# A gate on one queue: later loads issued once the first column's moments are computed

## The chip, the cores and the metric

The kernel runs on one core of a Trainium2 chip. The metric is the time of one execution on the device in microseconds, as the median of several executions. The profile is of one execution; its times are microseconds from the first instruction of the program.

## What is computed

The input x has 2048 rows of 512 bfloat16 values. Each row is normalised (mean and variance over its 512 values), and the result feeds two branches whose outputs are added to x:

```python
x = A_x
xn = _layernorm(x, axis=-1)
return x + _A_ref(xn, A_w_r, A_w_i) + _B_ref(xn, B_w_gate, B_w_up, B_w_down)
```

Branch A is a spectral filter: a real two-dimensional Fourier transform of xn, a product with the complex weights w_r + i w_i, and the inverse transform. Branch B is a gated feed-forward layer: g = xn w_gate and u = xn w_up (512 to 1792), h = gelu(g) * u, and h w_down (1792 to 512).

## The kernel before

The 2048 rows are held as 16 columns of 128 rows, one row of a column in each partition; row 16 p + c lies in partition p of column c. `x_t` holds the columns as loaded, `xn` the normalised ones, and `xnT` their transposes, which the matrix products read. `Wg_sb` and `Wu_sb` hold the gate and up weights as four blocks of 128 inputs by 1792 outputs.

For a column, DVE computes the moments (`f_stats`, L339, then `f_mean`, L342, into `mv`). The reciprocal root of the variance is made on ACT and DVE for columns 0 and 1, and on POOL for the others. DVE or ACT then writes `xn` (L345, L452). Columns 0 to 3 are transposed on TensorE (`f_T`, L351, into `tp`) and copied to `xnT` by DVE or ACT (L354); the other columns are transposed by DMA (L455).

The matrix products of branch B come in units (function `unit`): a unit covers some columns and some blocks of 128 outputs. It makes `g_ps` and `u_ps` on TensorE (L490; L498 for the gate half of the first unit), the gelu on ACT (L503) and the product on DVE (L508). The first two units take columns 0 and 1 one at a time with output blocks 0 to 3, which need the outputs 0 to 512 of both weight matrices; the third and fourth take columns 0 and 1 together with blocks 4 to 7, which need the outputs 512 to 1024. The products of branch A (`bp`, `dp`, `ep`, `gp`, `yp`) are spread between later units, and the products with `Wd_sb` (`y_ps`, L817) close the program. Before the first transposes TensorE runs 37 matmuls on a zero tile (L320), and six more (L324) before the first unit; their results are not used.

The order on each engine is fixed before the program runs. Most work is registered with `plan.add`, with an engine, an estimated duration, dependencies and a key; a small simulation (`Plan.order`) picks the next operation by earliest start and key, and the operations are then issued in that order. The loads at the top are not in the plan: they are issued directly, in the order of the text, on the queue of SP, and stand ahead of everything that the plan puts on SP. `load_x(c0, n)` (L273) loads n columns of x, `load_w(T, a, b)` (L277) loads outputs a to b of one weight matrix. At most eight DMAs on this queue have a semaphore of their own: a ninth waits for the landing of the first, and so on.

`first_two` registers the work on columns 0 and 1. Its helper `v` adds a DVE operation that follows the one added before it. Its first operations are:

```python
stats(0)
mean(0)
stats(1)

recip(0)
xn_(0, 0)
```

Of the kernel before, what the change touches and what calls it, by code (L numbers as in the profile page):

```python
# [19 lines left out]
NC = 16  # L20
NG = 8
NE = 4
DF = 1792
# [111 lines left out]
class Plan:  # L135
# [6 lines left out]
    def add(self, eng, occ, fn, deps=(), key=0.0, lat=None, slack=0.0, t_min=0.0, acq=(), rel=(), after=None):  # L142
        lat = occ + 0.25 if lat is None else lat
        op = Op(len(self.ops), eng, occ, lat, fn, [d for d in deps if d is not None], key, slack, t_min, acq, rel,
                after)
        self.ops.append(op)
        return op
# [54 lines left out]
def kernel(  # L202
# [11 lines left out]
    nc = tc.nc  # L214
    const_np, ccols, rf_np, ri_np, idx_np = _tables()
    cap = nc.inline_tensor(const_np, name="spec_consts").ap()
    rf_d = nc.inline_tensor(rf_np, name="spec_rf").ap()
# [12 lines left out]
    x_t = pc.tile([P, NC, D], BF16, name="x_t", tag="x_t")  # L230
    CT = pc.tile([P, const_np.shape[1]], BF16, name="CT")
    Wg_sb = pc.tile([P, NE, DF], BF16, name="Wg_sb")
    Wu_sb = pc.tile([P, NE, DF], BF16, name="Wu_sb")
# [4 lines left out]
    RF_t = pc.tile([P, NC, P], BF16, name="RF_t", tag="RF")  # L238
    late = {}
    W = 257  # L240
    TW = pc.tile([P, 2, 17, W], BF16, name="TW", tag="TW")
    TR, TI = TW[:, 0], TW[:, 1]
# [5 lines left out]
    def load_consts(first, last):  # L248
        a, b = ccols[first][0], sum(ccols[last])
        nc.sync.dma_start(out=CT[:, a:b], in_=cap[:, a:b])  # L250


    def load_x(c0, n, eng=nc.sync):
        eng.dma_start(out=x_t[:, c0:c0 + n, :], in_=x_v[:, c0:c0 + n, :])

    def load_w(a, b, eng=nc.sync):
        nc.sync.dma_start(out=Wg_sb[:, :, a:b], in_=wg_v[:, :, a:b])
        eng.dma_start(out=Wu_sb[:, :, a:b], in_=wu_v[:, :, a:b])
# [25 lines left out]
    nc.sync.dma_start(out=idx_t[:], in_=nc.inline_tensor(idx_np, name="spec_rows").ap())  # L284
    load_w(Wg_sb, 0, 512)
    load_w(Wu_sb, 0, 512)
    load_x(2, 2)
    load_w(Wg_sb, 512, 1024)
    load_w(Wu_sb, 512, 1024)
    load_x(4, 2)  # L290
    load_x(6, 2)
    load_w(Wg_sb, 1024, DF)
    load_w(Wu_sb, 1024, DF)
    load_x(8, 2)
    load_x(10, 2)
    for c in range(0, NC, 8):
        nc.sync.dma_start(out=RF_t[:, c:c + 8], in_=rf_d.rearrange("p (c k) -> p c k", c=NC)[:, c:c + 8])
    load_x(12, 2)
    load_x(14, 2)
    load_consts("F0", "L0")  # L300
    load_consts("I0", "M0")
    for T, w_in in ((TR, A_w_r), (TI, A_w_i)):
        rows = w_in.rearrange("(kb a h g) k -> h kb a (g k)", kb=NC, h=2, a=8)
        Tf = T.rearrange("p j k -> p (j k)")
        for h in range(2):
            nc.sync.dma_start(out=Tf[64 * h:64 * h + 64, W:8 * W], in_=rows[h, :, 0:4, W:8 * W])

    LAND = {0: 2.9, 1: 3.6, 2: 8.4, 3: 8.4}
    LAND.update({c: 11.5 if c < 8 else 17.5 if c < 12 else 20.5 for c in range(4, NC)})
# [18 lines left out]
    add = plan.add  # L328
    V, A, T_ = nc.vector, nc.scalar, nc.tensor
# [7 lines left out]
    def f_stats(c):  # L337
        tiles["st", c] = st = pw.tile([P, V.BN_STATS_DIM], F32, name="stats", bufs=4)
        V.bn_stats(out=st[:], in_=x_t[:, c, :])  # L339

    def f_mean(c):
        V.bn_aggr(out=mv[:, c, :], in_=tiles["st", c][:])  # L342

    def f_norm_v(c, o, w):
        V.tensor_scalar(out=xn[:, c, o:o + w], in0=x_t[:, c, o:o + w], scalar1=mv[:, c, 0:1],  # L345
                        scalar2=rstd[:, c:c + 1], op0=ALU.subtract, op1=ALU.mult)

    def f_T(c, e0, n):
        tiles["T", c, e0] = tp = ps.tile([P, n, P], BF16, name="tp", tag="S", bufs=4)
        for e in range(n):  # L350
            T_.transpose(tp[:, e], xn[:, c, (e0 + e) * P:(e0 + e + 1) * P], ident)  # L351

    def f_Tc(c, e0, n, copy=V.tensor_copy):
        copy(out=xnT[0][:, e0:e0 + n, c, :], in_=tiles["T", c, e0][:])  # L354
# [19 lines left out]
    def first_two():  # L374
        o = {}

        def v(k, fn, occ, deps=(), lat=None, t_min=0.0):
            o[k] = add("DVE", occ, fn, [o[d] for d in deps], key=-2000 + len(o), lat=lat, t_min=t_min,
                       after=o.get("last"))
            o["last"] = o[k]  # L380

        def T(c, h):
            o["T", c, h] = add("PE", 0.12, lambda: f_T(c, 2 * h, 2), [o["xn", c, h]], key=-2000 + 2 * c + h,
                               lat=0.36, acq=("S",))

        def xn_(c, h):
            v(("xn", c, h), lambda: f_norm_v(c, 256 * h, 256), 0.27, [("recip", c)], lat=0.4)

        def stats(c):
            v(("stats", c), lambda: f_stats(c), 0.6, t_min=LAND[c], lat=0.7)  # L390

        def mean(c):
            v(("mean", c), lambda: f_mean(c), 0.17, [("stats", c)])
            o["root", c] = add("ACT", 0.31, lambda: A.activation(
                out=rstd[:, c:c + 1], in_=mv[:, c, 1:2], func=AF.Sqrt, bias=eps_t[:], scale=1.0),
                [o["mean", c]], key=-2000 + c)

        def recip(c):
            v(("recip", c), lambda: V.reciprocal(out=rstd[:, c:c + 1], in_=rstd[:, c:c + 1]), 0.15, [("root", c)])

        stats(0)
        mean(0)
        stats(1)

        recip(0)
        xn_(0, 0)
        mean(1)
        xn_(0, 1)
        T(0, 0)
        T(0, 1)  # L410
        add("PE", 0.33, spin_on, [o["T", 0, 1]], key=-1500, lat=0.33, after=o["T", 0, 1])
        table = add("ACT", 1.3, lambda: None, [o["root", 1]], key=-1500, lat=1.3)
        v("copy0", lambda: f_Tc(0, 0, 2), 0.25, [("T", 0, 0)], lat=0.4)
        o["copy0"].rel = ("S",)
        xT_op[0, 0] = o["copy0"]
        recip(1)
        v("copy1", lambda: f_Tc(0, 2, 2), 0.25, [("T", 0, 1)], lat=0.4)
        o["copy1"].rel = ("S",)
        xT_op[0] = o["copy1"]
        xn_op[0] = o["xn", 0, 1]  # L420
        v("xn1", lambda: f_norm_v(1, 0, D), 0.33, [("recip", 1)], lat=0.45)
        t = add("PE", 0.23, lambda: f_T(1, 0, NE), [o["xn1"]], key=-1998, lat=0.45, acq=("S",))
        o["t"] = t
        v("copyt", lambda: f_Tc(1, 0, NE), 0.5, ["t"])
        o["copyt"].rel = ("S",)
        xT_op[1] = o["copyt"]
        xn_op[1] = o["xn1"]

    ROOT = 1.1
    first_two()  # L430

    def moments(c, key):
# [448 lines left out]
```

## Time and profile before

| | |
|---|---|
| median of six runs | 178.75 us (178.48 to 179.11) |
| the profiled execution, its own time | 178.66 us |
| its span, first to last instruction | 177.0 us |
| TensorE busy | 173.0 us |
| DVE busy | 116.2 us |
| ACT busy | 96.0 us |
| POOL busy | 17.2 us |
| bytes moved by DMA | 19.35 MB |

In the profile PE is TensorE's matmuls and PEld its weight loads, which overlap them. SPq is the instruction stream of SP, which issues the loads. A group line gives the program's line, the engine, the operation and its tiles. In a timeline the first two numbers are start and length of a row, and the bracket says how long the engine stood idle before it and what ended that. The profiled execution's own time is 1.66 us longer than its span; that part lies outside the instructions.

The first loads were issued by SP at 0.80 (columns 0 and 1 of x), 1.71 (a table of row numbers), 2.18 (gate weights 0 to 512) and 2.65 (up weights 0 to 512). Columns 2 and 3 followed at 3.20, the second gate quarter (512 to 1024) at 3.75 and the second up quarter at 4.23.

### The profile page before, as it was taken

How to read it: one execution, taken by the hardware profiler on the slowest of the kernel's cores; microseconds unless marked ns; L12 is line 12 of the kernel's file. 1: busy time of each engine (PE TensorE's matmuls, PEld its weight loads, DVE VectorE, ACT ScalarE, POOL GpSimd, SP SyncE). 2: the span in 40 equal slices, each digit the busy share in tenths (PEclk: the TensorE clock that was granted, in tenths of full speed). 3: DMA queues.
4: the chain of work that ended last, by engine and by line, in shares of the span. 5: the costliest groups of instructions: out<-in, count | busy, mean ns of one | idle time of the engine just before them, and what ended most of it. 6: DMA issues, size and time to landing. Idle time of an engine off the chain costs nothing.

```text
span 177.0 us, 3132 instructions
## 1 busy us (share of the span) xinstructions
PE 173.0 (98%) x1145; PEld 97.1 (55%) x1145; DVE 116.2 (66%) x255; ACT 96.0 (54%) x170; POOL 17.2 (10%) x38
## 2 busy tenths in 40 slices
PE   7999999999999999999999999999999999999993
PEld 7898845455545554555455455454445445444463
DVE  3678999987434599979899999643516325345333
ACT  4442489799736988898899964362112111211200
POOL 1020340505760000000000000000000000000000
PEclk9999999999999999999999999999999999999999
DMA  3999999335716802211201520200132221221212
GB/s 82 357 374 378 376 188 143 67 63 70 254 35 228 309 0 59 59 30 35 59 19 43 147 51 15 59 0 4 59 90 89 77 75 61 89 88 60 78 45 59
DMA packets 21871, 19.35 MB, mean 109 GB/s; under 512 B 8480, under 2 KB 20000, under 8 KB 21856
## 3 DMA queue, kind: packets, MB, share of 16 engines
q1 hardware_dynamic: 21440, 17.84, 36.5%
q0 software_dynamic: 416, 1.32, 2.6%
q8 instruction: 9, 0.15, 0.4%
q14 instruction: 6, 0.05, 0.1%
HBM read 13.38 MB, written 2.10 MB: 87 GB/s over the span
## 4 chain that ended last, share of the span: by engine, by line
PE 94%; DMA 3%; SPq 1%; issue 0%; DVE 0%
PE u_ps L490 27%; PE y_ps L817 27%; PE g_ps L490 27%; DMA Wu_sb<-in_B_w_up_dram 3%; PE bp L577 2%; PE yp L768 2%; PE gp L738 2%; PE dp L635 2%; PE y_ps L821 2%; PE ep L644 2%; SPq L273 0%; PE tp L351 0%; SPq L277 0%; SPq L284 0%; DVE y_sb L824 0%
## 5 line engine op out<-in xcount | busy, mean ns | idle before, releaser
L490 PE MATMUL u_ps<-xnT,Wu_sb 128*128 128x512 bf16 (+2 forms) x272 | 57.3, 341 | 0.1
L490 PE MATMUL g_ps<-xnT,Wg_sb 128*128 128x512 bf16 (+2 forms) x256 | 56.2, 349 | 0.0
L817 PE MATMUL y_ps<-Wd_sb,hT 128*128 128x512 bf16 (+2 forms) x252 | 51.1, 355 | 0.0
L508 DVE TENSOR_TENSOR hT<-u_ps,ge 128x512 bf16<-128x512 f32 x56 | 38.5, 689 | 18.2 <-PE u_ps L490 14.5
L503 ACT ACTIVATE ge<-g_ps 128x512 bf16<-128x512 f32 x56 | 33.7, 602 | 24.0 <-PE g_ps L490 21.3
L490 PEld LDWEIGHTS <-Wu_sb 128*128 128x128 bf16 x272 | 24.9, 98 | 20.9 <-DMA Wu_sb<-in_B_w_up_dram 0.2
L817 PEld LDWEIGHTS <-hT 128*128 128x128 bf16 x252 | 23.2, 98 | 22.4
L490 PEld LDWEIGHTS <-Wg_sb 128*128 128x128 bf16 x256 | 24.0, 98 | 20.6
L774 ACT CAST yf<-yp 128x512 bf16<-128x512 f32 x16 | 9.3, 587 | 40.5 <-PE yp L768 40.5
L824 DVE TENSOR_TENSOR y_sb<-y_ps,y_sb 128x512 bf16<-128x512 f32 (+2 forms) x18 | 11.1, 631 | 30.0 <-PE y_ps L821 30.0
L649 ACT CAST E<-ep 64x512 bf16<-64x512 f32 x32 | 18.6, 580 | 1.4 <-PE ep L644 1.0
L339 DVE BATCH_NORM_STATS2 stats<-x_t 128x6 f32<-128x512 bf16 x16 | 10.4, 677 | 2.5 <-DMA x_t<-in_A_x_dram 2.4
L452 ACT ACTIVATE xn<-x_t,nb,rstd 128x512 bf16<-128x512 bf16 x12 | 9.5, 815 | 1.0 <-POOL nb L370 1.0
L547 ACT CAST ds<-dp 128x512 bf16<-128x512 f32 x16 | 9.2, 598 | 0.8 <-PE dp L635 0.8
L547 ACT CAST Gs<-gp 128x512 bf16<-128x512 f32 x16 | 8.7, 592 | 0.6 <-PE gp L738 0.5
L547 ACT CAST Bs<-bp 128x512 bf16<-128x512 f32 x16 | 8.3, 609 | 0.5 <-PE bp L577 0.5
L780 DVE TENSOR_TENSOR lv<-yf 128x512 bf16<-128x512 bf16 x16 | 6.1, 422 | 1.5 <-ACT yf L774 0.6
L768 PEld LDWEIGHTS <-Gs 128*128 128x128 bf16 x64 | 4.8, 98 | 3.5
L787 DVE TENSOR_TENSOR yt<-lv 128x512 bf16<-128x512 bf16 x16 | 6.1, 421 | 0.3
L821 PE MATMUL y_ps<-yt,RI_t 128*128 128x512 bf16 (+2 forms) x18 | 6.1, 355 | 0.0
L768 PE MATMUL yp<-CT,Gs 128*128 128x128 bf16 x64 | 6.0, 219 | 0.0
L559 DVE TENSOR_TENSOR A<-xn 128x1024 bf16<-128x1024 bf16 x8 | 5.2, 677 | 1.0 <-ACT xn L452 1.0
(65 smaller groups left out, 120.3 us busy)
## 6 DMA issues: line engine op xcount, KB each, us to landing
F<-F SPq DMA_DIRECT2D x32, 64.0 KB, 2.0
y_sb<-in_A_x_dram SPq DMA_DIRECT2D x16, 128.0 KB, 2.1
out_dram<-y_sb SPq DMA_DIRECT2D x15, 128.0 KB, 1.7
x_t<-in_A_x_dram SPq DMA_DIRECT2D x7, 256.0 KB, 8.8
Wd_sb<-in_B_w_down_dram SPq DMA_DIRECT2D x1, 1792.0 KB, 7.6
Wg_sb<-in_B_w_gate_dram SPq DMA_DIRECT2D x2, 512.0 KB, 5.4
Wu_sb<-in_B_w_up_dram SPq DMA_DIRECT2D x2, 512.0 KB, 6.4
Wg_sb<-in_B_w_gate_dram SPq DMA_DIRECT2D x1, 768.0 KB, 10.1
```

The source lines that it names most:

```text
L339: V.bn_stats(out=st[:], in_=x_t[:, c, :])
L452: xn_op[c] = add("ACT", 0.72, lambda c=c: A.activation(out=xn[:, c, :], in_=x_t[:, c, :], func=AF.Identity, bias=nb[:, c:c + 1], scale=rst ...
L490: T_.matmul(b[name][:, f], lhsT=W_[:, e, (f0 + f) * P:(f0 + f + 1) * P], rhs=rhs[:, e, :], start=(e == 0), stop=(e == NE - 1))
L503: A.activation(out=b["ge"][:], in_=b["g_ps"][:], func=AF.Gelu_apprx_tanh)
L508: V.tensor_tensor(out=hT_of(sb, f0, m, o, w), in0=b["u_ps"][:], in1=b["ge"][:], op=ALU.mult)
L547: A.copy(out=o, in_=i)
L649: A.copy(out=b["E"][64 * h:64 * h + 64, r], in_=b["ep", h][64 * r:64 * r + 64])
L768: T_.matmul(t[:, q], lhsT=late["G"][:, q, c0 + j], rhs=IQ[q], start=(q == 0), stop=(q == 3), skip_group_check=True)
L774: A.copy(out=b["yf"][:, j], in_=b[j][:])
L817: T_.matmul(b[o][:], lhsT=hT_of(sb, f, 1, cl * P, P)[:, 0], rhs=Wd_sb[:, f, o:o + w], start=(f == 0), stop=False)
L821: T_.matmul(b[o][:], lhsT=late["RI"][:, c, :], rhs=late["yt"][:, c, o:o + w], start=False, stop=True)
L824: V.tensor_tensor(out=b["y"][:, o:o + w], in0=b[o][:], in1=b["y"][:, o:o + w], op=ALU.add)
```

## The change

All loads behind the first quarter of the up weights are moved into a function, unchanged and in the same order. That function is registered in the plan as one SP operation, which depends on a new DVE operation: a memset of one element of `x_t`, in column 2, placed between the mean of column 0 and the statistics of column 1. Column 2 is the first thing that the moved loads write, so the first of them waits for the memset. In the instruction streams DVE has one instruction more, the load of columns 2 and 3 has one wait more, and all else stands in the order of before.

```diff
     load_w(Wg_sb, 0, 512)
     load_w(Wu_sb, 0, 512)
-    load_x(2, 2)
-    load_w(Wg_sb, 512, 1024)
-    load_w(Wu_sb, 512, 1024)
-    load_x(4, 2)
-    load_x(6, 2)
-    load_w(Wg_sb, 1024, DF)
-    load_w(Wu_sb, 1024, DF)
...
+
+    def later_loads():
+        load_x(2, 2)
+        load_w(Wg_sb, 512, 1024)
+        load_w(Wu_sb, 512, 1024)
+        load_x(4, 2)
+        load_x(6, 2)
+        load_w(Wg_sb, 1024, DF)
+        load_w(Wu_sb, 1024, DF)
+        load_x(8, 2)
+        load_x(10, 2)
+        for c in range(0, NC, 8):
+            nc.sync.dma_start(out=RF_t[:, c:c + 8], in_=rf_d.rearrange("p (c k) -> p c k", c=NC)[:, c:c + 8])
+        load_x(12, 2)
+        load_x(14, 2)
+        load_consts("F0", "L0")
+        load_consts("I0", "M0")
+        for T, w_in in ((TR, A_w_r), (TI, A_w_i)):
...
         stats(0)
         mean(0)
+        v("gate", lambda: V.memset(x_t[0:1, 2, 0:1], 0.0), 0.06, lat=0.1)
+        add("SP", 9.0, later_loads, [o["gate"]], key=-1000)
         stats(1)
```

More of the change, by code (lines that the diff above doesn't have):

```diff
@@ L286 @@
     load_w(Wu_sb, 0, 512)
-    load_x(2, 2)
-    load_w(Wg_sb, 512, 1024)
-    load_w(Wu_sb, 512, 1024)
-    load_x(4, 2)
-    load_x(6, 2)
-    load_w(Wg_sb, 1024, DF)
-    load_w(Wu_sb, 1024, DF)
[L294 to L306, printed above, removed]
+    def later_loads():
[15 more added lines that the diff above has]
+        for T, w_in in ((TR, A_w_r), (TI, A_w_i)):
+            rows = w_in.rearrange("(kb a h g) k -> h kb a (g k)", kb=NC, h=2, a=8)
+            Tf = T.rearrange("p j k -> p (j k)")
+            for h in range(2):
+                nc.sync.dma_start(out=Tf[64 * h:64 * h + 64, W:8 * W], in_=rows[h, :, 0:4, W:8 * W])
     LAND = {0: 2.9, 1: 3.6, 2: 8.4, 3: 8.4}
```

## The prediction

> **What bounds the kernel now.** I read the page first, for which engine carries the span and what the chain that ended last consists of.
>
> ```profile
> span 177.0 us, 3132 instructions
> PE 173.0 (98%) x1145; PEld 97.1 (55%) x1145; DVE 116.2 (66%) x255; ACT 96.0 (54%) x170; POOL 17.2 (10%) x38
> ...
> PE 94%; DMA 3%; SPq 1%; issue 0%; DVE 0%
> ```
>
> TensorE is the bound. Ahead of its work in the chain stands one DMA piece, 3% of the span. The chain in order of time, cut to 0 to 14 us, shows where that lies:
>
> ```profile
> 2.18 0.43 SPq L277
> 2.61 0.04 issue
> 2.65 5.20 DMA Wu_sb<-in_B_w_up_dram
> 7.85 0.05 issue
> 7.89 1.07 PE u_ps L490 x16
> ```
>
> So the first quarter of the up weights (issued at 2.65, landed at 7.85) lets TensorE go at 7.89, and from there the chain holds almost only TensorE work. A microsecond won or lost there moves the end one for one; what lands later without stopping TensorE costs nothing. The timeline says how much TensorE really lost there, and what is next to stop it:
>
> ```profile
> 7.86 0.42 DVE L354 COPY xnT<-tp 128x512 bf16<-128x512 bf16 x1 [1.21 <-PE tp L351]
> 7.89 0.90 PEld L490 LDWEIGHTS <-Wu_sb 128*128 128x128 bf16 x16 [0.24 <-DMA Wu_sb<-in_B_w_up_dram]
> ...
> 8.61 0.69 DVE L339 BATCH_NORM_STATS2 stats<-x_t 128x6 f32<-128x512 bf16 x1 [0.32 <-DMA x_t<-in_A_x_dram]
> ...
> 10.53 1.68 PEld L490 LDWEIGHTS <-Wg_sb 128*128 128x128 bf16 x16
> ```
>
> The weight loader idled 0.24 us before the first up matmul: that is all an earlier landing can give back. The next two loads on the path are the ones that the change puts behind its gate: x columns 2 and 3 (DVE starts on them at 8.61) and the second quarter of the gate weights (first used at 10.53). Then the DMA issues, each taken alone, with microseconds from issue to landing; x_t was issued at 3.20 and Wg_sb at 3.75:
>
> ```profile
> x_t<-in_A_x_dram SPq DMA_DIRECT2D x1, 256.0 KB, 5.4
> Wg_sb<-in_B_w_gate_dram SPq DMA_DIRECT2D x1, 512.0 KB, 6.6
> ```
>
> They land at 8.60 and 10.35: DVE takes the x columns at once, and the gate weights have 10.53 - 10.35 = 0.18 us to spare. Last the windows, to see whether issue or bandwidth sets those landings (last two columns: busy share of the DMA engines, and GB/s):
>
> ```profile
> 4.00:5.00 1.00, 1.00 (x12) 0.91 (x9) 0.88 (x3) 0.30 (x1) 0.00 (x0) 1.00 0.79 248
> 5.00:6.00 1.00, 0.90 (x8) 0.53 (x7) 0.83 (x5) 0.63 (x2) 0.00 (x0) 1.00 1.08 377
> 6.00:7.00 1.00, 1.00 (x15) 0.96 (x14) 0.65 (x4) 0.95 (x1) 0.00 (x0) 1.00 1.07 380
> 7.00:8.00 1.00, 0.93 (x17) 0.76 (x15) 0.14 (x1) 0.36 (x1) 0.00 (x0) 1.00 1.06 340
> ```
>
> From about 4.5 us the DMA engines are full. The windows from 1 to 7 us move 20 + 233 + 50 + 248 + 377 + 380 = 1308 kB. The x columns 0 and 1 and the first gate and up quarters are 2 x 128 + 2 x 512 KB = 1311 kB. So those bytes, and hardly any of a load behind them, had moved by 7.0: the loads go through in the order of their issue. What stands behind the gate is not touched by the engines before about 7.0, and Wg_sb's second quarter not before 7.0 + 262 kB / 377 GB/s = 7.7.
>
> **The change part by part.**
>
> The gate: one DVE memset of one element. The 128x1 memsets (L264, L266) take 0.06 us, the 128x64 one 0.11. It stands between the first column's mean (3.80 + 0.18 = 3.98) and the second column's statistics, which start at 4.09 because their column lands only at 1.25 + 2.8 = 4.05. The 0.11 us hole covers it: 0 on DVE. Without that cover it would push the DVE chain of columns 0 and 1 by 0.06 to 0.11 us; that chain feeds transposes and matmuls that are done 0.24 us before the up weights come, so still 0 at the end.
>
> The wait: SP finishes the up issue at 2.65 + 0.51 = 3.16 and now waits for the memset's end, about 4.04 to 4.09. The trace has one such release, a 1x1 memset on POOL that ends at 53.01 with the DMA behind it issued at 53.05, so 0.04 us more: x columns 2 and 3 go out at about 4.10 instead of 3.20, 0.9 us later. Queued behind on SP, in unchanged order, are the second quarters of Wg and Wu, the other x loads, the weight thirds, RF_t, CT, TW, and then the transposes (from 22.28) and everything later. At the spacing of before, Wg_sb's second quarter goes out at 3.75 + 0.9 = 4.65 and Wu_sb's at 5.13. The issues are back in step by 10: at 6.67 and 8.04 SP sat 1.33 and up to 1.83 us on single issues where earlier ones took 0.43 to 0.68, held by a full queue, and the RF_t issue at 10.39 waits for a landing anyway. No other engine issues a load in this stretch, and all other instructions keep their order.
>
> What the 0.9 us costs: the delayed loads must reach the engines before these run dry at 7.0. For the time from issue to first bytes the nearest row is Wd_sb, issued into an idle queue at 53.05: the window 53.50:54.00 shows 0 GB/s and 54.00:54.50 shows 68, so between 0.95 and 1.45 us; 285 GB/s is reached in 55.00:55.50, within 2.45 us. x columns 2 and 3, out at 4.10, have bytes ready by 5.55 and need them at 7.0: 1.4 us to spare. Wg_sb's second quarter has them by 6.1 and needs them at 7.7: 1.6 us to spare. By this, 0 us lost. The other end is the whole 0.9 us sliding through to the landings, priced below. I take 0, since the engines keep a backlog of 1311 - 325 (moved by 4.1) = about 990 kB, 2.6 us at 377 GB/s, against 0.9 of delay.
>
> What it gains: between 0 and 0.24 us. Less traffic behind the up weights could let them land earlier, but the sum above shows hardly any of that traffic moving before 7.0, and it will be queued again by 5.55. I take 0.
>
> The Trainium skill, "DMA: Bandwidth & Descriptors", section "Rules for kernel authors", speaks against the change: issue a DMA early and wait for it late, so that its fixed cost overlaps. By that rule alone holding the issue back costs up to the 0.9; this trace covers it with a backlog. The same page, section "Specifications", gives about 0.6 us to first byte for DMAs of this path; by it the sum is 0 as well, with more to spare; the 0.95 to 1.45 us here are longer, and they are what counts. Its section "Queues, rings and completion order" says that each DMA engine consumes descriptors in ring order, which is what the 1308 of 1311 kB show here; by it the gain is 0.
>
> Sum: 178.66 us (the profiled execution, span 177.0 and 1.66 around it) + 0 + 0 - 0 = 178.66. The median of the six runs is 0.09 higher; I forecast 178.7.
>
> **The rivals.**
>
> The delay slides through (slower). If bytes come more than 3.05 us after issue (7.7 - 4.65), or the queue doesn't catch up, the second gate quarter lands up to 0.9 later, 11.25, and the weight loader, which wants it at 10.53, waits 0.72. The x columns land at 9.50, their normalised columns move from 12.19 (11.46 + 0.73) to up to 13.09, and the transposes, which TensorE would by then start at 12.22 + 0.72 = 12.94, wait another 0.15. Price 0.72 to 0.87, say 0.8: 179.5. It decides once the second gate quarter is over 0.18 us late. For it: DVE and TensorE take both loads almost as they land. Against it: the backlog.
>
> The up weights land earlier (faster). For it: some DMA engines run ahead, and the bytes from 6.5 to 7.5 belong partly to x columns 2 and 3 while the last up rows land at 7.85. Gain at most the 0.24 us gap, then the copy at 7.86 to 8.28, the x columns and the gate weights (0.18 to spare) come next: 178.42, or 178.5 against the median. That is 0.13%, less than can be told.
>
> The change doesn't do what it says: it holds back issues, and the transfers behind them were waiting for the engines anyway. That is my forecast.
>
> **How the numbers follow.** A measurement of this kernel can tell about 0.2% (0.36 us): the six runs lie from 178.48 to 179.11, 0.15% under to 0.20% over their median. Hidden, 178.7: 0.72. Earlier landing, 178.5: 0.13. Slide through, 179.5: 0.12. Something else, either way: 0.03. By cases: hidden gives 0.64 same and 0.04 on each side by scatter; earlier landing 0.05 faster, 0.08 same; slide 0.11 slower, 0.01 same; the rest 0.01 each. Faster 0.10, same 0.74, slower 0.16. The range runs from the earlier landing less 0.2 us of scatter, 178.3, to the slide's 179.5.
>
> **What the next profile would show.** Right: the L273 issue of columns 2 and 3 near 4.1; the up weights landing at 7.8 to 7.9 with a PEld gap of about 0.24; x columns landing near 8.6; the second gate quarter by 10.5; the windows 5 to 10 still at 340 to 380 GB/s; RF_t issued near 10.4. Wrong: a window between 6 and 9 under 300 GB/s, a PEld gap on Wg_sb before 10.6 or on xn near 12.2 (slide), or an up landing before 7.7 with the gap gone (gain).

## The result, and the profile after

The changed kernel is slower: 179.7 us in the median of 28 runs, against 179.02 us of the kernel before on the same chips; ratio 1.0049, 95% interval 1.0035 to 1.0062. Executions at a lower granted clock are left out of the ratio, as one of the changed kernel at 0.991. The ratio is worth 0.9 us. The median lies outside the range of 178.3 to 179.5; carried over to the 178.75 us that the forecast started from, the ratio gives 179.6, just outside as well. The profiled execution took 179.51 us, of which 177.8 are the span.

The page first, as before:

```profile
span 177.8 us, 3133 instructions
PE 173.3 (97%) x1145; PEld 97.1 (55%) x1145; DVE 116.0 (65%) x256; ACT 96.0 (54%) x170; POOL 17.6 (10%) x38
...
PE 88%; DMA 5%; DVE 2%; ACT 2%; issue 1%; SPq 0%
```

TensorE works as long as before (173.3 against 173.0 us), in a span 0.8 us longer. The chain now holds more DMA, and DVE and ACT pieces that it did not have. Its first part, in order of time:

```profile
0.80 2.13 DMA x_t<-in_A_x_dram
2.93 0.02 issue
2.95 0.71 DVE stats L341
3.66 0.02 issue
3.68 0.18 DVE mv L344
3.86 0.03 DVE stats L341
3.90 0.02 issue
3.92 0.34 SPq L273
4.26 0.04 issue
4.30 6.75 DMA Wg_sb<-in_B_w_gate_dram
11.04 0.05 issue
11.09 1.92 PE g_ps L494 x16
```

The gate stands in the chain: first column, statistics, mean, memset (the piece at 3.86 carries the line of the statistics that overlap it), the released issue at 3.92, the second gate quarter, landed at 11.04 instead of 10.34. The weight loader's list of waits says what that costs, and shows a second loss in another place:

```profile
PEld L494 <- DMA Wg_sb<-in_B_w_gate_dram: 0.5, 1, 0.5
PEld L494 <- DMA Wu_sb<-in_B_w_up_dram: 0.4, 1, 0.4
...
PEld L581 <- issue: 0.2, 1, 0.2
```

The first is the loader's wait ahead of the third unit, which TensorE starts at 11.09 instead of 10.59: **0.50 us**. The second is not a loss: the up weights land at 7.85 as before, and the loader is ready 0.2 us sooner. The third lies at 41.2 us, in branch A. The 33rd to 48th `bp` matmuls, in the timelines of TensorE of the kernel before (first line) and after:

```profile
39.70 1.06 PE L577 MATMUL bp<-RF_t,xf 128*128 128x128 bf16 x16
```

```profile
40.22 1.39 PE L581 MATMUL bp<-RF_t,xf 128*128 128x128 bf16 x16
```

They begin 0.52 us later, which is the first loss, and last **0.33 us** longer. 0.50 + 0.33 = 0.83 of the 0.85 us between the spans (177.80 and 176.95 unrounded); what follows is late by the same amount to the end.

**The first loss** is in the transfers. Windows (busy share of the DMA engines, GB/s):

```profile
6.00:7.00 1.00, 1.00 (x16) 0.74 (x14) 0.35 (x2) 0.65 (x1) 0.00 (x0) 1.00 1.21 357
7.00:8.00 1.00, 0.73 (x14) 0.56 (x12) 0.34 (x1) 0.56 (x1) 0.00 (x0) 1.00 0.79 235
8.00:9.00 1.00, 1.00 (x20) 1.00 (x20) 0.09 (x1) 0.04 (x1) 0.00 (x0) 1.00 0.93 284
9.00:10.00 1.00, 1.00 (x22) 1.00 (x20) 0.67 (x2) 0.11 (x1) 0.00 (x0) 1.00 1.06 353
```

Against 340 GB/s before, 7 to 8 us moves 235. The next window moves 284; before it was:

```profile
8.00:9.00 1.00, 1.00 (x20) 1.00 (x20) 0.68 (x2) 0.24 (x1) 0.00 (x0) 1.00 1.03 347
```

Taken together the engines had not run dry: the 2 KB packets of x columns 2 and 3 begin at 6.70 us in both traces. But the busy share falls with the rate (0.79 and 0.93 against 1.06 and 1.03). Added up from the start and length of each packet in the trace, about 17 packets are in flight at any time from 5.5 to 6.5 us in both kernels. From 6.75 to 8.75 us, in steps of 0.25, it is 13.4 to 15.7 after and 15.7 to 17.3 before. With fewer than 16 in flight, some of the 16 engines have nothing to move; that begins where the first loads come to their end. And single packets are slow: ten of the 2 KB packets take over 200 ns, the longest 1045 ns (median 84 ns); before, three do, the longest 324 ns.

A load has landed when the last of the 16 steps that its semaphore makes has come. For the second gate quarter the ninth step comes at 10.14 us (9.81 before) and the last at 11.04 (10.34): the load is not only later, its parts lie further apart. So the columns land at 9.31 instead of 8.59 (DVE's wait for them is now 1.25 us, 0.32 before), and the gate quarter behind them 0.7 us late.

**The second loss** starts on DVE at 25 us. Timeline of DVE, kernel before and after:

```profile
24.33 0.66 DVE L559 TENSOR_TENSOR A<-xn 128x1024 bf16<-128x1024 bf16 x1
25.23 0.69 DVE L508 TENSOR_TENSOR hT<-u_ps,ge 128x512 bf16<-128x512 f32 x1 [0.24 <-PE u_ps L490]
```

```profile
24.85 0.66 DVE L563 TENSOR_TENSOR A<-xn 128x1024 bf16<-128x1024 bf16 x1
26.17 0.69 DVE L512 TENSOR_TENSOR hT<-u_ps,ge 128x512 bf16<-128x512 f32 x1 [0.66 <-ACT xn L456]
```

The sum of xn's halves begins 0.52 us late, the product that writes `hT` 0.94. Its `u_ps` was done at 25.64 and its gelu at 25.42, so by its waits it could start near 25.74, 0.1 us after `u_ps` as before; it starts 0.43 us after that. The releaser named, ACT's `xn`, is only what happened to end last: the programs wait for the same counts in both kernels, apart from DVE's own count, one higher (for this product ACT's 17th step, which came with the gelu at 25.43; `xn` is the 18th). Nor is it the POOL instruction of 1.04 us that runs meanwhile: it begins at 25.17 before and at 25.68 after, and before, the product started beside it without a delay. From this product the delay goes to the statistics behind it, to POOL's `nb`, to ACT's `xn` (groups: 1.0 us idle before, 1.8 after, all on `nb`), and to ACT's copies of `bp` out of PSUM, 0.94 us late. A `bp` matmul then waits for a buffer.

### The profile page after: what moved, and what is told of

Same layout as the page of the kernel before. It is cut to its first block, busy times and chain, and to the rows that moved or that the text cites. A ratio compares the mean times of both kernels' runs of the same rounds, so it can differ in the third digit from the quotient of the medians.

```text
span 177.8 us, 3133 instructions
## 1 busy us (share of the span) xinstructions
PE 173.3 (97%) x1145; PEld 97.1 (55%) x1145; DVE 116.0 (65%) x256; ACT 96.0 (54%) x170; POOL 17.6 (10%) x38
## 4 chain that ended last, share of the span: by engine, by line
PE 88%; DMA 5%; DVE 2%; ACT 2%; issue 1%; SPq 0%
PE y_ps L821 27%; PE g_ps L494 25%; PE u_ps L494 25%; DMA Wg_sb<-in_B_w_gate_dram 4%; PE yp L772 2%; PE gp L742 2%; PE dp L639 2%; PE y_ps L825 2%; PE ep L648 2%; PE bp L581 1%; DMA x_t<-in_A_x_dram 1%; ACT Bs L551 1%; DVE hT L512 1%; DVE A L563 1%; ACT ge L507 1%
```

## The experiments

"Landing distance" below is the time from the landing of the first up quarter to that of the second gate quarter, from each profile: 2.49 us before, 3.19 us after. The bp stretch is the start of the 33rd to that of the 48th bp matmul: 0.84 us before, 1.17 us after.

**First set: the wait, its place, and the loads behind it.**

e1, gate opened at the start:

```diff
+        v("gate", lambda: V.memset(x_t[0:1, 2, 0:1], 0.0), 0.06, lat=0.1)
+        add("SP", 9.0, later_loads, [o["gate"]], key=-1000)
         stats(0)
         mean(0)
-        v("gate", ...)
-        add("SP", 9.0, later_loads, [o["gate"]], key=-1000)
```

> The same memset and the same wait, but the memset stands ahead of the first statistics, where DVE has nothing to do, so the gate is open at about 1.1 us and no load is held back. Theory S (a load's bytes follow its issue by a fixed few us, so the held-back issue slides through to the landing): issue of x columns 2 and 3 at 3.20, landing at 8.6, second gate quarter landing at 10.3 to 10.4, time as before within 0.2%. Rival W (the memset or the wait itself costs, whenever it opens): landings of 9.3 and 11.0 as in the changed kernel, time 0.4 to 0.5% over before.

Measured: 1.0016 (1.0002 to 1.0029). The x columns go out at 3.20, landing distance 2.49: nothing left of the first loss. The bp stretch is 1.16 us: the second loss stays. So the first loss comes from when the loads go out, and the second comes with gate, wait or memset.

e2, gate behind `xn_(0, 1)`:

```diff
         mean(1)
         xn_(0, 1)
+        v("gate", lambda: V.memset(x_t[0:1, 2, 0:1], 0.0), 0.06, lat=0.1)
+        add("SP", 9.0, later_loads, [o["gate"]], key=-1000)
```

> The gate moves from behind the first column's mean to behind the second half of its normalisation, so the held-back loads go out at about 5.4 instead of 3.9. Theory S (slide, one for one): x columns 2 and 3 land about 1.5 later than in the changed kernel, near 10.8, the second gate quarter near 12.5, TensorE stands 1.8 to 2.1 us before it, time about 1.5 us over the changed kernel, 181.2. Rival R (the DMA engines run empty once after the up weights and pay one restart of fixed length, whatever the delay): landing of the second gate quarter under 11.5, time within 0.4 us of the changed kernel.

Measured: 1.0036 (1.0021 to 1.0051). The x columns go out at 5.80, 1.9 us later than in the changed kernel, and land at 9.10, sooner than there, although the up quarter itself landed late, at 8.20; landing distance 3.05. A delay of 2.6 us costs no more than one of 0.7: the delay does not slide through. Windows of e2:

```profile
7.00:8.00 1.00, 1.00 (x20) 0.99 (x18) 0.00 (x0) 0.17 (x2) 0.00 (x0) 1.00 1.05 236
8.00:9.00 1.00, 0.92 (x17) 0.76 (x15) 0.42 (x1) 0.58 (x1) 0.00 (x0) 1.00 0.87 216
```

The same dip, from 7 to 8 us at a busy share of 1.05, as high as in the kernel before: here the slow packets count for more. Eighteen of the 2 KB packets take over 200 ns, the longest 975.

e3, the three next loads ahead of the gate, gate (on x column 4) behind `copy1`:

```diff
+    load_x(2, 2)
+    load_w(Wg_sb, 512, 1024)
+    load_w(Wu_sb, 512, 1024)
     def later_loads():
-        load_x(2, 2)
-        load_w(Wg_sb, 512, 1024)
-        load_w(Wu_sb, 512, 1024)
```

> x columns 2 and 3 and the second quarters of both weights go out ahead of the gate; the gate holds the loads of x columns 4 on and opens behind the second transpose copy, near 6.4, so x columns 4 and 5 go out about 1.4 later than the 4.96 of before, with over 1.5 MB queued ahead of them. Theory S with a fixed latency of 3 to 3.7 us from issue to first bytes: bytes at about 10, when the queue gets there, so no dry window: x columns 4 and 5 land at 12.4 to 12.8, windows 9 to 13 stay over 340 GB/s, time as before within 0.2%. Rival D (every delay of an issue slides through, however much is queued): landing near 13.9, a window between 9 and 12 under 300 GB/s; the time may still be that of before, since these columns are first used at 15.4.

Measured: 1.0029 (1.0001 to 1.0058). x column 4 goes out 1 us later than before (5.97) and lands at 12.53, before 12.48; landing distance 2.21. By the landings, a held load further back costs nothing. The bp stretch is 1.16, so the second loss is there.

e7, x columns 2 and 3 free, the rest held until `xn_(0, 1)`:

```diff
+    load_x(2, 2)
     def later_loads():
-        load_x(2, 2)
...
+        v("gate", lambda: V.memset(Wg_sb[0:1, 0, 512:513], 0.0), 0.06, lat=0.1)
```

> x columns 2 and 3 are issued ahead of the gate (3.20 as before); the gate opens behind the second half of the first normalisation, so the second gate quarter goes out near 5.8 instead of 3.75, 2 us late. Theory R: the restart moves from x columns 2 and 3 to the second gate quarter, which has 0.18 us to spare; x columns land at 8.6, the gate quarter at 10.6 to 11.2, time 0.1 to 0.5% over before. Theory S (slide): gate quarter at 12.4, time 1.1% over before. If a backlog of the x columns alone covers 2 us, landing 10.4 and time as before.

Measured: 1.0013 (1.0000 to 1.0025). The second gate quarter goes out at 5.49 instead of 3.75, about 2 us ahead of its first packets, and lands at 10.30 (before 10.34); landing distance 2.20, no 2 KB packet over 109 ns, and windows without a dip:

```profile
7.00:8.00 1.00, 0.94 (x17) 0.77 (x14) 0.02 (x1) 0.24 (x1) 0.00 (x0) 1.00 1.05 364
8.00:9.00 1.00, 0.86 (x16) 0.86 (x17) 0.59 (x2) 0.36 (x1) 0.00 (x0) 1.00 1.09 351
```

So, of the loads held in these runs, only the one directly behind the up quarter must not be late. It isn't the number of bytes still queued: 805 kB were when e7's quarter went out, and 1017 kB when the x columns of the changed kernel did.

e5, the changed kernel again. 

> The changed kernel itself, on one chip with the three variants beside it, for a size to compare them with: 0.35 to 0.6% over before. Theory R (restart: what costs is that the DMA engines come to the end of the up weights with nothing fetched behind them, a cost of some 0.7 us that hardly grows with the delay) and theory S (slide) both expect that.

Measured: 1.0062 (1.0031 to 1.0093), landing distance 3.17, bp stretch 1.15: both losses repeat.

e6, no gate, no memset; two small loads hold SP instead:

```diff
     load_w(Wu_sb, 0, 512)
+    for k in range(2):
+        tiny = pc.tile([1, 3], I32, name=f"tiny{k}")
+        nc.sync.dma_start(out=tiny[:], in_=...)
     load_x(2, 2)
```

> The kernel before with no gate, no memset and no wait, but two loads of 12 bytes each issued between the up quarter and x columns 2 and 3, so that SP issues these at about 4.0 to 4.1, as late as in the changed kernel. Theories R and S: the delay alone is enough, slow windows at 7 to 9 us (under 300 GB/s), second gate quarter landing near 11, time 0.3 to 0.6% over before. Rival W (the memset or the wait costs): time within 0.2% of before.

Measured: 1.0057 (1.0036 to 1.0077), landing distance 3.85, more than the gate's. The bp stretch is 0.84: without the memset there is no second loss.

e8, the loads as before, and only a memset into a scratch tile where the gate memset stands. 

> The kernel before with the one-element memset in the same place, into a tile that nothing reads; loads issued directly as before. Theories R and S: time within 0.15% of before. Rival W, memset half: over 0.2% slower.

Measured: 1.0017 (1.0004 to 1.0030), bp stretch 1.15. One memset of one element costs 0.3 us, and not where it stands. The loads go out as before, and yet this profile has a landing distance of 2.83 us and windows of 312 and 289 GB/s from 7 to 9 us: a part of the dip is scatter from one execution to the next. DVE at 25 us in e8, with nothing else changed:

```profile
24.43 0.66 DVE L562 TENSOR_TENSOR A<-xn 128x1024 bf16<-128x1024 bf16 x1
25.73 0.69 DVE L511 TENSOR_TENSOR hT<-u_ps,ge 128x512 bf16<-128x512 f32 x1 [0.65 <-ACT xn L455]
```

e4, the kernel before with the `idx_t` load issued last. 

> The kernel before with one move: the load of the row numbers (idx_t, first used by POOL near 42 us) is issued last instead of third, so that every load behind it goes out 0.47 us earlier; no gate. Theory S: gate quarter lands at 5.9, up quarter at 7.4, x columns 2 and 3 near 8.1, second gate quarter near 9.9; the 0.24 us gap before the first up matmul goes, and the time falls by 0.2 to 0.25 us (0.12%). Rival Q (landings are set by bandwidth, not by issue): landings earlier by 0.1 at most, time as before.

Measured: 0.9978 (0.9967 to 0.9989), faster than both kernels. Each later load goes out about 0.47 us earlier, the first up matmul starts 0.1 us earlier (7.79). The landings come close to the second expectation (x columns at 8.55, with 208 GB/s from 7 to 8 us, second gate quarter at 10.18), but the time falls, and by more than the first had. The profile's span is 0.1 us shorter; where the rest of the 0.4 us is won is not shown.

**Second set: what one memset costs.**

e9, two memsets instead of one:

```diff
         mean(0)
+        v("m0", lambda: V.memset(mark[0:1, 0:1], 0.0), 0.06, lat=0.1)
+        v("m1", lambda: V.memset(mark[0:1, 1:2], 0.0), 0.06, lat=0.1)
         stats(1)
```

> The kernel before with two one-element DVE memsets between mean(0) and stats(1), into a scratch tile; loads as before. It asks what the 0.3 us is that each kernel with one more DVE instruction lost near 25 us (33rd to 48th bp matmul 1.15 to 1.17 us, against 0.83 to 0.84 us without it). Place theory (P): the instruction's place in DVE's stream counts: with one more, the multiplication that writes hT falls on a place where its start is held 0.4 us, with two more it has passed that place; the 33rd to 48th bp matmul take 0.84 us again, and the kernel agrees with the kernel before within 0.15%. Work theory (W): the added DVE work or its semaphore count costs the time: at least 1.15 us again there, 1.0015 to 1.004 of the kernel before.

Measured: 0.9984 (0.9959 to 1.0009), bp stretch 0.84. Twice the work costs nothing:

```profile
25.34 0.69 DVE L511 TENSOR_TENSOR hT<-u_ps,ge 128x512 bf16<-128x512 f32 x1 [0.24 <-PE u_ps L493]
```

e10, one memset directly behind that product:

```diff
             V.tensor_tensor(out=hT_of(sb, f0, m, o, w), in0=b["u_ps"][:], in1=b["ge"][:], op=ALU.mult)
+            if k == 9:
+                V.memset(mark[0:1, 0:1], 0.0)
```

> The kernel before with one one-element DVE memset directly behind the hT multiplication that is held in the kernels with the early memset (10th unit, near 25.9 us). P: everything up to that multiplication keeps its place, so no hold there: 33rd to 48th bp matmul 0.84 us, ratio 0.9990 to 1.0010. W: one more DVE instruction in the same stretch, about 0.06 us later from there on; if the count or the work is what costs, 1.15 us and 1.0015 or more.

Measured: 0.9993 (0.9967 to 1.0019), bp stretch 0.84.

e11, the changed kernel with another memset taken from DVE:

```diff
-    nc.vector.memset(minus_half[:], -0.5)
+    nc.gpsimd.memset(minus_half[:], -0.5)
```

> The changed kernel with the memset of minus_half moved from DVE to POOL, so DVE has as many instructions ahead of the 25 us stretch as in the kernel before; the gate memset and the wait of SP's queue stay. P: the hold near 25 us is gone (33rd to 48th bp matmul 0.84 us) while the second gate quarter still lands near 11.0 us: what is left is the DMA part alone, 1.0015 to 1.0035 of the kernel before (about +0.5 us less what slack takes). W: both parts stay, 1.0045 to 1.0065.

Measured: bp stretch 0.84 with gate, wait and late loads in place, so the second loss is gone. The first is there (landing distance 3.49, wait on the gate quarter 0.8 us). The time, 1.0048 (1.0013 to 1.0083), did not come down by 0.3 us as it should have: the runs lie from 178.97 to 181.05, and in the profiled one the first column landed at 3.18 and so the gate opened 0.24 us later. The profile carries this verdict, the time does not.

**Third set: what makes the first load behind slow.**

e12, the second gate quarter ahead of the x columns in the moved function. 

> The changed kernel with the order of the first two loads behind the gate swapped: the second gate quarter first (issue near 3.9 us), x columns 2 and 3 behind it (near 4.5 us). If the load directly behind the running up quarter is the one that is slowed whatever it is, the stretch from 7 to 9 us shows under 310 GB/s again, with packets of the gate quarter of half a microsecond and more, and the x columns land near 9.6 to 10.0 us. If it is the 2 KB packets of the x columns that are slow, the gate quarter runs at 350 GB/s or more from 6.9 us and lands by 9.2 us, and the x columns behind it show the long packets. Time: the third gate unit then waits for x columns or not at all; 1.000 to 1.007.

Measured: 1.0079 (1.0053 to 1.0105). The expectation missed how the kernel works: the memset writes `x_t`, so the gate quarter, now first, did not wait and went out at 3.20, and only the x columns were held (4.01). It landed at 9.20 and they at 9.90, 2.19 us behind the up quarter for both, with 352 and 358 GB/s from 7 to 9 us: no dip, and no 2 KB packet over 285 ns. The weight loader waited 1.0 us for the columns' normalised values, and TensorE stood 0.72 us.

e14, the same order with the gate on the quarter, and a second memset for the place on DVE:

```diff
-        v("gate", lambda: V.memset(x_t[0:1, 2, 0:1], 0.0), 0.06, lat=0.1)
+        v("gate", lambda: V.memset(Wg_sb[0:1, 0, 512:513], 0.0), 0.06, lat=0.1)
+        v("m1", lambda: V.memset(mark[0:1, 0:1], 0.0), 0.06, lat=0.1)
```

> The changed kernel with the second gate quarter ahead of x columns 2 and 3 and the gate memset on that quarter, so that the quarter is issued near 3.95 us directly behind the up weights; one more small DVE memset keeps the held multiplication off its place (33rd to 48th bp matmul 0.84 us). If the load directly behind is slowed whatever it is (B): 7 to 9 us under 310 GB/s in the mean, quarter landed 9.6 to 10.0 us instead of 9.2 us, x columns 10.3 to 10.8 us; the transposes of columns 2 and 3 then wait 1.3 to 2 us, 1.006 to 1.011. If the 2 KB packets of the x columns were the cause (X): 7 to 9 us at 350 GB/s or more, quarter at 9.2 us, x columns at 9.9 us, the wait 1.0 us and 1.004 to 1.007.

Measured: 1.0115 (1.0100 to 1.0131); bp stretch 0.84. The quarter, out at 3.95, lands at 9.90 instead of 9.20, the columns at 11.23, 3.58 us behind the up quarter: slowed whatever stands there, and the columns behind it too. From 7 to 9 us it moves 301 and 328 GB/s, a little more than expected. (The profile is of an execution of 182.52 us, 2 us over the median; only its loads and the bp stretch are read.)

e13, e6 with one small load. 

> The kernel before with one 12-byte load between the first up weights and x columns 2 and 3, no gate, no memset: x columns issued near 3.6 us, half way between the kernel before (3.2) and the changed one (3.9). If the loss grows with lateness from the first moment (G): x columns land 0.3 to 0.5 us later than the 8.6 us of before, ratio 1.001 to 1.003. If there is a point between 3.6 and 3.9 us from which the load is slowed (K): landing as before within 0.2 us, ratio 0.999 to 1.001. If the extra load itself, and not the lateness, costs (the small packets in the stream): as much as with two, x columns near 9.9 us, 1.004 to 1.007.

Measured: 1.0070 (1.0056 to 1.0084), as much as with two, although the columns went out at 3.65. The profile is of the shortest of five executions; there the dip shows (229 and 283 GB/s from 7 to 9 us), but the landing distance is only 2.91 and the columns land at 8.84.

e15 and e16, one and two small loads in the kernel with `idx_t` last, and e17, that kernel alone. 

> The kernel with idx_t last, and one 12-byte load between the first up weights and x columns 2 and 3: up weights issued at 2.2 us, x columns at 3.2 us as in the kernel before. If the absolute issue time decides (A): as the kernel with idx_t last, second gate quarter 2.2 to 2.8 us behind the up quarter, 0.997 to 0.999 of the kernel before. If the distance behind the issue of the up weights or the extra load decides (D): 2.9 us or more, 1.002 to 1.005, 0.4 us and more over the kernel with idx_t last.

> The kernel with idx_t last, and two 12-byte loads between: x columns issued near 3.65 us. A: slowed as in e13, 2.9 us or more between the landings, 1.001 to 1.004 (0.2 us less than e13, since the up weights are earlier). D: slowed as in e6, 1.002 to 1.005. If neither shows a loss here, an issue of 3.65 us is early enough and what e13 lost has another reason.

> The kernel before with the idx_t load issued last, again, beside e15 and e16 on their chip: 0.9967 to 0.9989 as in e4.

Measured: e15 1.0019 (0.9997 to 1.0042), e16 1.0052 (1.0029 to 1.0075), e17 0.9971 (0.9950 to 0.9992; median 178.36 us, the best of all). In e15 the columns go out at 3.19, as in the kernel before, and yet its median is 0.9 us over e17's. Its profile doesn't show where: it is of the shortest execution (178.71, median 179.26), with a landing distance of 2.85 and windows of 243 and 327 GB/s from 7 to 9 us. e16, out at 3.45, has a landing distance of 3.94, more than any gate. So the small loads seem to cost something themselves, beside the later issue of what follows, and these runs don't separate the two. What e6 showed is therefore not the delay alone, as it had seemed, and the runs with small loads can't tell whether the time of the issue by the clock matters.

## Why the prediction was wrong

All profiles in one table, without those with small loads between, and without e4, for which the profile names no up landing (by the steps of its semaphores it would stand in the first row, with 2.43 and 0.48):

| the load directly behind the up quarter | kernels | landing distance of the two loads behind, us | last step of the second one behind its ninth, us |
|---|---|---|---|
| issued at 2.7 to 3.2 | before, e1, e3, e7, e8, e9, e10, e12, e17 | 2.49, 2.49, 2.21, 2.20, 2.83, 2.44, 2.47, 2.19, 2.50 | 0.53, 0.38, 0.41, 0.68, 0.68, 0.51, 0.38, 0.25, 0.64 |
| held, issued at 3.9 to 5.8 | after, e5, e11, e2, e14 | 3.19, 3.17, 3.49, 3.05, 3.58 | 0.91, 1.33, 1.71, 0.83, 1.55 |

**The failed step: "x columns 2 and 3, out at 4.10, have bytes ready by 5.55 and need them at 7.0: 1.4 us to spare ... By this, 0 us lost".** Being there in time is true of the first packets: they start at 6.70, as before (so they were needed a little sooner than at 7.0). The conclusion is false: being there in time is not enough. The two loads take 0.7 us longer (medians 2.47 and 3.19). The sum took the engines together, either fed or dry. In the traces they are less filled at the handover to the held load: from 6.75 to 7.00 us 15.1 to 16.6 packets are in flight in the five held kernels, 16.9 to 17.7 in the nine others. And the last parts of the load lag, as the last column shows; e5's second gate quarter has its ninth step at 9.62, sooner than in the kernel before, and its last at 10.95. The backlog of 990 kB hid the delay of the first packets and not this. Of the 0.7 us TensorE pays 0.50, since the gate quarter had 0.18 to spare.

Slow packets alone don't account for it. The changed kernel has one of 1045 ns, but e5, with the same loss, none of 2 KB over 402, while e10 has one of 459 without a loss.

**The second: the gate memset, "0 on DVE".** In its own place that was right, though not through the hole of 0.11 us, which wasn't there (the second column landed at 3.45 instead of 4.07): in the trace after, the memset lies under the statistics of the second column. But it cost 0.33 us at 41 us, where the prediction had no term. Eight profiles with exactly one DVE instruction more ahead of 25 us (after, e1, e2, e3, e5, e7, e8, e12) have bp stretches of 1.14 to 1.17 us; eleven with none or two more (before, e4, e6, e9, e10, e11, e13, e14, e15, e16, e17) have 0.84. Shown is that the instruction's place in DVE's stream decides, and neither its work nor the gate. Counted in the program as built, with its wait instructions, the held product becomes the 65th instruction of DVE's stream, first after a multiple of 64; it is the 64th before and the 66th in e9. That the 64 matters is not shown: no start near the 129th, 193rd, 257th or 321st is held in the changed kernel and not before. What happens at the product the trace does not show either: no packet of the instruction queues lies between 23 and 27.5 us.

**The wait.** Right in kind; SP was released 0.05 us after the end of the memset, at 3.92 and not 4.10: 0.12 of the difference because the first column landed at 2.93 instead of 3.05, the rest because the memset ran beside the statistics. The x columns were 0.72 us late, the gate quarter 0.55.

**The gain, taken as 0.** Right: the up weights landed at 7.85 in both; over the runs of the table that issue them at 2.65, from 7.65 to 8.20 with the next load held and from 7.62 to 8.15 without.

**The rival "slides through".** Two of its three signs came (a window under 300 GB/s, a loader's wait on the gate quarter that begins before 10.6; none on `xn` near 12.2), and its 179.5 us is close to 179.7. But its mechanism was wrong, and its size right by chance: it priced a wait of 0.72 where 0.51 was measured, and 0.15 for the transposes, which did not wait; the other 0.33 came from DVE. By it, e2's loads would have had to land 2 us later than the changed kernel's; the x columns landed 0.2 us sooner, the gate quarter 0.2 us later. The Trainium skill, "DMA: Bandwidth & Descriptors", section "Rules for kernel authors", says to issue early and wait late. These runs agree for the load directly behind: 0.50 us were lost although 2.6 us of queued bytes were there to cover a fixed cost.

**What stays open.** Why the engines are less filled and the last parts lag when the load directly behind is issued late, and from which delay on. It isn't the lead alone (e7's gate quarter had some 2 us and ran undisturbed, the x columns of the changed kernel nearly 3 and did not), not the bytes queued (e7), not the kind of packets (e14). Each landing distance is from one execution, and e8 shows that without a change it can reach 2.83. A restart of the queues after a pause would fit e2 and e14, but e7 and e3 pause too, one load further back, without a loss. In the changed kernel, with just two large loads queued at the pause, it hurts; with three queued it does not: that is what the runs separate, and no more. Why the place in DVE's stream costs 0.43 us is open too.

## What to carry to other kernels

Count the loads queued behind the one that is running, not only the bytes: here a backlog of 2.6 us did not cover holding back the very next load by 0.7 us, while holding back the one behind it by 1.7 us left its landing as it was. A load is there when its slowest part is, so look at the last parts and not only at the rate. When a single added instruction costs time far from where it stands, add a second one or move it to another engine before explaining it by its work: here two memsets cost nothing and one cost 0.3 us. A gain lay on the other side: the small table that nobody needs early, issued last, lets the first weights go out 0.46 us sooner and gives 0.2 to 0.3%.

## What the runs showed of the hardware

- A busy share near 1 of the DMA engines is no proof of their rate: 236 GB/s at a share of 1.05 (e2), against 377 at 1.08 in the kernel before. Single 2 KB packets took up to 1045 ns where the median is 84.
- The last of a load's 16 steps can lag far behind the others: in e5 the fifteenth of x columns 2 and 3 came at 8.43 us and the last at 9.44.
- A load of 12 bytes between two large ones is not free: one put 0.9 us on the median (e15 against e17), two 1.6 us (e16), with the later issue of the loads behind in it (0.46 and 0.72 us).
- A DVE instruction can start 0.4 us later after its inputs, by its place in the stream alone: 0.52 us after `u_ps` in the kernels with one instruction more, 0.10 in those with none or two.
